# Two attention-and-feed-forward blocks on one core: the first unit of weights alone split and multiplied beside the attention, with the heads' work laid out anew

## The chip, the cores and the metric

The kernel runs on one core of a Trainium2 chip. The time is device time in microseconds, the median of several executions. The engines are named as in the profile: PE (TensorE), PEld (its weight loads), DVE (VectorE), ACT (ScalarE), POOL (GpSimd), and SP, whose queue issues the transfers.

## What is computed

Causal attention over 2 batches of 12 heads, 448 tokens and 64 channels each, then two feed-forward blocks on the 896 tokens by 768 channels that come out of it. The weights arrive as 64-bit floating point numbers. Shortened:

```
scores = scale * matmul(q, k.T);  scores = where(upper triangle, -1e9, scores)
attn = softmax(scores);  x = matmul(attn, v)            # heads side by side: 896 x 768
x = (silu(x @ w_gate) * (x @ w_val)) @ w_out            # 768 -> 1536 -> 768
h = x @ w_in;  out = maximum(h, 0)**2 @ w_out2          # 768 -> 2048 -> 768
```

## The kernel before, in words

**Weights.** The weights are cut into 68 units of 128 rows by 768 columns: g and v by turns (gate and value, 12 of each), then o, h and f. A unit is loaded as 64-bit words (`load_w`, tile wraw) by a transfer on SP, and split by `split_w` into a high part whi and a low part wlo, each a type that PE multiplies in one pass. The split has nine steps, each one instruction: step 0 the absolute value of the high words (ACT, tile wa), step 1 a clamp (DVE), 2 a shift (DVE), 3 a merge with the sign (DVE), 4 rounding to whi (ACT), 5 a mask (DVE, tile wr), 6 a scaling of the low words (DVE), 7 a subtraction (DVE), 8 the sum that gives wlo (DVE). There are two buffers of wa, one of wr, three pairs of whi and wlo.

**Three multiplications.** `mm3` multiplies one block of a unit with one block of tokens three times: high by high, high weight by low token part, low weight by high token part. Given two batches it does each of the three for both batches before it goes to the next. Tokens' parts are ahi and alo. A unit on one batch is 18 multiplications, on both 36.

**Attention.** The heads go in 12 pairs. For a pair `stage_at` transposes q and k on PE and `stage_copy` copies them on ACT; `score_mm` multiplies them on PE in two halves; `score_max` (DVE) and `score_exp` (ACT), four chunks to a head; `guard` (POOL), `recip` (DVE), `normalise` (POOL, four chunks; DVE for the first two heads); `transpose_p` (PE, in two groups), `transpose_out` (one group on ACT, one on DVE); `values` (PE), and its result goes to ahi (`channels_hi`, ACT) and alo (`channels_lo`, DVE).

**Order.** Every engine works through its instructions in the order in which they are written. In the attention that order comes from a planner: `attention_plan` lists the operations with an engine, a cost of the planner's own, what each follows and which buffers it takes, and `Plan.run` places them one by one by their start and a rank. The ranks are the head's number plus an offset from the table RANK. The constant NEARLY says how many units of weights the plan holds whole: for each the load (W), the nine steps (J), the multiplications on the first batch (G, `early_mm`, tile early) and a copy of their result to SBUF (GC, `early_out`, on ACT). Of one unit more, the load and steps 0 to 3 are in the plan.

**Behind the attention** the order is the written one. The main loop calls `gate_or_val` for g and v by turns: for the first NEARLY units on the second batch alone, since the first is there already, for all others on both batches. Before it uses a unit, `unit` sees to it by `split_to` that this one and the next are split. The steps of one unit and the first steps of the next stand by turns there:

```
elif n == NEARLY:
    split_w(n, 4)
after = start_w()
if after is not None:
    split_w(after, 0)
...
for z, y in ((5, 1), (6, 2), (7, 3), (8, 4)):
    split_w(n, z)
    if after is not None:
        split_w(after, y)
```

Between them `follow_up` puts the instructions that finish earlier units: sigmoids, products, splits of results.

Of the kernel before, what the change touches and what calls it, by code (L numbers as in the profile page):

```python
# [23 lines left out]
MASKED = -8.0e9  # L24

C = 112
NEARLY = 2


RANK = {  # L30
# [4 lines left out]
}  # L35

QUEUED = 1130
# [6 lines left out]
class Warmth:  # L44

    W, LEAST, FROM = 10240 / 3, 3060, 24000
# [19 lines left out]
class Plan:  # L66
# [9 lines left out]
    def add(self, key, engine, cost, after=(), takes=(), uses=(), rank=0, later=0, cols=0):  # L76


        later += 200 if engine == "PE" else 120
        self.ops[key] = (engine, cost, tuple(after), tuple(takes), rank, later, cols)  # L80
        for t in (*takes, *uses):
            self.users.setdefault(t, []).append(key)
# [69 lines left out]
def attention_plan(NP, NPAIR, NC, S, U, KD, rank=RANK):  # L152
# [59 lines left out]

    for n in range(NEARLY + 1):
        r = rank["J"] + n
        raw, a, b, ws = ("wraw", n), ("wa", n), ("wr", n), ("ws", n)
        add(("W", n), "SP", 2200, [("LD", n, 1)], [raw], [], rank["W"] + 2 * n, 2500)
        for z in range(9 if n < NEARLY else 4):
            engine, cost, takes, uses = (
# [4 lines left out]
            add(("J", n, z), engine, cost, [("J", n, z - 1)] if z else [("W", n)], takes, uses, r)  # L223
        if n >= NEARLY:
            continue
# [33 lines left out]
def tile_attention_moe_moe(ctx, tc, q, k, v, w_gate, w_val, w_out, w_in2, w_out2, out):  # L259
# [131 lines left out]
    def start_w():  # L391
        n = state["start"]
        if n < NU:
            load_w(n + 3)
            state["start"] += 1
            return n

    def split_to(upto):

        while state["split"] < min(upto, NU):  # L400
            n = state["split"]
            if state["start"] == n:
                for z in range(5):
                    split_w(start_w() if z == 0 else n, z)
            elif n == NEARLY:
                split_w(n, 4)
# [213 lines left out]
    def gate_or_val(kind, m, bs):  # L620
        hi, lo = unit(kind, m, 0)
        pss = {b: bank(kind) for b in bs}
        for kk in range(KD):
            c = slice(kk * 128, (kk + 1) * 128)
            mm3(pss, hi[:, c], lo[:, c], x_hi[kk], x_lo[kk], kk == 0, kk == KD - 1)
        return pss
# [42 lines left out]
    with tc.manual_schedule():  # L669
# [43 lines left out]
        for m in range(KF1):  # L713
            for kind in "gv":
                ps = gate_or_val(kind, m, [1] if n < NEARLY else [0, 1])
                if n < NEARLY:
                    ps[0] = early[n]
# [118 lines left out]
```

## Time and profile before

| | |
|---|---|
| median of 3 runs | 604.18 us (604.11 to 604.2) |
| profiled execution | 604.23 us, of which the span from the first to the last instruction is 602.1 |
| PE busy | 594.5 us, 99% of the span |
| DVE busy | 473.5 us, 79% |
| ACT busy | 284.1 us, 47% |
| POOL busy | 89.9 us, 15% |

Times in the profile count from the start of the span. The attention takes the first sixth of it: the last value product begins at 95.68 us. An instruction's duration begins when it is started and ends when its result is there, so that two neighbours on one engine can overlap; the distance from one start to the next is then what an instruction takes of its engine.

### The profile page before, as it was taken

How to read it: one execution, taken by the hardware profiler on the slowest of the kernel's cores; microseconds unless marked ns; L12 is line 12 of the kernel's file. 1: busy time of each engine (PE TensorE's matmuls, PEld its weight loads, DVE VectorE, ACT ScalarE, POOL GpSimd, SP SyncE). 2: the span in 40 equal slices, each digit the busy share in tenths (PEclk: the TensorE clock that was granted, in tenths of full speed). 3: DMA queues.
4: the chain of work that ended last, by engine and by line, in shares of the span. 5: the costliest groups of instructions: out<-in, count | busy, mean ns of one | idle time of the engine just before them, and what ended most of it. 6: DMA issues, size and time to landing. Idle time of an engine off the chain costs nothing.

```text
span 602.1 us, 8832 instructions
## 1 busy us (share of the span) xinstructions
PE 594.5 (99%) x3258; PEld 531.4 (88%) x3259; DVE 473.5 (79%) x839; ACT 284.1 (47%) x556; POOL 89.9 (15%) x154
## 2 busy tenths in 40 slices
PE   8999999999999999999999999999999999999997
PEld 5676667999999999999999999999999999999997
DVE  4878983999999999999977776888888888649741
ACT  5999983433333333333422224666666642222301
POOL 4566871211111111111000000000000000000000
PEclk9999999999999999999999999999999999999999
DMA  8795210333333333333433333333333335334202
GB/s 169 162 243 116 75 54 1 106 104 106 104 106 106 104 106 108 106 111 115 139 104 106 104 106 104 107 106 104 106 104 106 104 107 157 105 132 138 85 1 93
DMA packets 80779, 65.06 MB, mean 108 GB/s; under 512 B 34912, under 2 KB 76640, under 8 KB 80736
## 3 DMA queue, kind: packets, MB, share of 16 engines
q1 hardware_dynamic: 79808, 64.27, 36.6%
q8 instruction: 26, 0.43, 0.3%
q10 hardware_dynamic: 928, 0.23, 0.2%
q14 instruction: 17, 0.14, 0.1%
HBM read 61.73 MB, written 2.75 MB: 107 GB/s over the span
## 4 chain that ended last, share of the span: by engine, by line
PE 84%; ACT 0%; issue 0%; ACTq 0%
PE o L786 19%; PE h L616 7%; PE h L614 7%; PE h L618 7%; PE y L614 5%; PE y L618 5%; PE y L616 5%; PE g L618 5%; PE v L618 5%; PE v L614 5%; PE g L614 5%; PE v L616 5%; PE g L616 5%; PE early L614 0%; PE early L616 0%; PE early L618 0%
## 5 line engine op out<-in xcount | busy, mean ns | idle before, releaser
L374 ACT ACTIVATE whi<-wa 128x768 fp32r<-128x768 f32 x68 | 57.6, 847 | 177.3 <-DVE wa L371 134.8
L786 PE MATMUL o<-whi,b 128*128 128x384 f32 x336 | 85.6, 334 | 0.0
L362 DVE TENSOR_SCALAR wa<-wa 128x768 f32<-128x768 f32 x68 | 41.2, 606 | 46.4 <-ACT wa L359 46.4
L371 DVE SCALAR_TENSOR_TENSOR wa<-wraw,wa 128x768 uint32<-128x768 uint32 x68 | 75.6, 1112 | 0.0
L359 ACT ACTIVATE wa<-wraw 128x768 f32<-128x768 f32 x68 | 61.6, 906 | 17.8 <-DVE wlo L387 17.8
L387 DVE TENSOR_TENSOR wlo<-wa,wr 128x768 fp32r<-128x768 f32 x68 | 65.4, 961 | 0.1
L384 DVE TENSOR_TENSOR wa<-wa,whi 128x768 f32<-128x768 f32 x68 | 64.6, 951 | 0.4 <-ACT whi L374 0.4
L381 DVE SCALAR_TENSOR_TENSOR wr<-wraw,wr 128x768 f32<-128x768 uint32 x68 | 64.6, 951 | 0.1
L786 PEld LDWEIGHTS o<-whi,b 128*128 128x128 f32 x336 | 60.8, 188 | 0.0
L786 PE MATMUL o<-wlo,b 128*128 128x384 f32 x168 | 56.1, 334 | 0.0
L614 PE MATMUL h<-b,whi 128*128 128x448 f32 x192 | 55.2, 368 | 0.0
L618 PE MATMUL h<-b,wlo 128*128 128x448 f32 x192 | 55.2, 368 | 0.0
L709 POOL TENSOR_TENSOR b<-u,b 128x448 fp32r<-128x448 f32 x24 | 29.0, 1208 | 159.9 <-ACT b L708 159.9
L554 POOL TENSOR_SCALAR P<-P,st 128x448 f32<-128x448 f32 (+1 forms) x88 | 48.7, 571 | 11.6 <-DVE st L546 4.8
L536 ACT ACTIVATE P<-P,st 128x320 f32<-128x320 f32 (+2 forms) x96 | 47.7, 500 | 3.1 <-DVE st L530 1.5
L530 DVE CUSTOM_DVE_ANT_0 P<-s,mask 128x448 f32<-128x448 f32 (+2 forms) x96 | 35.2, 410 | 13.9 <-PE s L515 12.7
L614 PE MATMUL y<-b,whi 128*128 128x448 f32 x144 | 41.4, 368 | 0.0
L616 PE MATMUL y<-b,whi 128*128 128x448 f32 x144 | 41.4, 368 | 0.0
L618 PE MATMUL y<-b,wlo 128*128 128x448 f32 x144 | 41.4, 368 | 0.0
L614 PE MATMUL g<-ahi,whi 128*128 128x448 f32 x138 | 40.2, 368 | 0.0
L614 PE MATMUL v<-ahi,whi 128*128 128x448 f32 x138 | 40.2, 368 | 0.0
L618 PE MATMUL g<-ahi,wlo 128*128 128x448 f32 x138 | 40.1, 368 | 0.0
(98 smaller groups left out, 1152.4 us busy)
## 6 DMA issues: line engine op xcount, KB each, us to landing
wraw<-in_moe_w_out_dram SPq DMA_DIRECT2D x28, 768.0 KB, 4.4
wraw<-in_moe_w_in_dram SPq DMA_DIRECT2D x16, 768.0 KB, 4.6
wraw<-in_moe_w_gate_dram SPq DMA_DIRECT2D x12, 768.0 KB, 4.4
wraw<-in_moe_w_val_dram SPq DMA_DIRECT2D x12, 768.0 KB, 4.4
raw<-in_q_dram SPq DMA_DIRECT2D x24, 112.0 KB, 3.0
out_dram<-osb SPq DMA_DIRECT2D x14, 192.0 KB, 1.9
raw<-in_k_dram SPq DMA_DIRECT2D x22, 112.0 KB, 2.8
v<-in_v_dram SPq DMA_DIRECT2D x24, 96.0 KB, 2.7
```

The source lines that it names most:

```text
L359: nc.scalar.activation(out=af, in_=high.bitcast(F32), func=AF.Abs)
L371: nc.vector.scalar_tensor_tensor(out=a, in0=high, scalar=0xC0000000, in1=a, op0=ALU.bitwise_and, op1=ALU.bitwise_or)
L374: nc.scalar.activation(out=split_t[n][0], in_=af, func=AF.Copy)
L381: nc.vector.scalar_tensor_tensor(out=rf, in0=low, scalar=2.0 ** -52, in1=rf, op0=ALU.mult, op1=ALU.mult)
L384: nc.vector.tensor_tensor(out=af, in0=af, in1=split_t[n][0].bitcast(F32), op=ALU.subtract)
L387: nc.vector.tensor_tensor(out=split_t[n][1], in0=af, in1=r[0].bitcast(F32), op=ALU.add)
L536: nc.scalar.activation(out=a, in_=a, func=AF.Exp, scale=-1.0, bias=st(0), accum_out=st(1))
L554: (nc.vector if n_on_dve(h) else nc.gpsimd).tensor_scalar(out=o, in0=a, scalar1=st(2), scalar2=1.0, op0=ALU.mult, op1=ALU.mult)
L614: nc.tensor.matmul(out=pss[b][:, :S], lhsT=hi, rhs=mhi[:, halves(b)], start=first, stop=False)
L616: nc.tensor.matmul(out=pss[b][:, :S], lhsT=hi, rhs=mlo[:, halves(b)], start=False, stop=False)
L618: nc.tensor.matmul(out=pss[b][:, :S], lhsT=lo, rhs=mhi[:, halves(b)], start=False, stop=last)
L786: nc.tensor.matmul(out=pss[t][:, :N], lhsT=a[f][:, tk], rhs=w[:, c], start=f + n == 0, stop=f == KF2 - 1 and n == 2)
```

## The change

NEARLY goes from 2 to 1, and the table RANK gets other offsets. So the plan holds unit 0 whole and unit 1 up to step 3, in place of units 0 and 1 whole and unit 2 up to step 3. Unit 1's multiplications on the first batch, the copy of their result, and its steps 4 to 8, leave the plan, as do unit 2's load and steps 0 to 3. The main loop then multiplies unit 1 with both batches. Shortened to the two constants and the first line of the table:

```diff
-NEARLY = 2
+NEARLY = 1
...
-    "RA": 190.39, "AT": 2.52, "AC": -48.88, "S": -178.65, "SI": -278.69, "VJ": -5.38,
+    "RA": 348.64, "AT": 2.02, "AC": -96.22, "S": -383.35, "SI": -307.19, "VJ": -150.17,
```

In the rows below, lines of the changed kernel are lower by one. On DVE, the end of the attention and the first instructions behind it, before: COPY is the transposed probabilities' second group, alo4 and alo5 are `channels_lo` of pairs 10 and 11, wa_1213 and wr_1532 are unit 2's tiles, wa_1526 is unit 3's.

```order
L584 COPY pt_1374<-pt_1369 128x512
L371 SCALAR_TENSOR_TENSOR wa_1213<-wraw_608,wa_1213 128x768
L605 TENSOR_TENSOR alo4_87<-x_1378,ahi4_81 128x448
L584 COPY pt_1406<-pt_1400 128x512
L605 TENSOR_TENSOR alo5_88<-x_1415,ahi5_82 128x448
L377 TENSOR_SCALAR wr_1532<-wa_1213 128x768
L362 TENSOR_SCALAR wa_1526<-wa_1526 128x768
L381 SCALAR_TENSOR_TENSOR wr_1532<-wraw_608,wr_1532 128x768
L367 TENSOR_SCALAR wa_1526<-wa_1526 128x768
L704 TENSOR_TENSOR sg_1528<-early_1436,sg_1528 128x448
L384 TENSOR_TENSOR wa_1213<-wa_1213,whi_1521 128x768
L371 SCALAR_TENSOR_TENSOR wa_1526<-wraw_1498,wa_1526 128x768
```

The same place after: wa_786 and wr_1471 are unit 1's tiles, wlo_1461 its low part, wa_1469 is unit 2's.

```order
L545 RECIPROCAL st_150<-st_150 128x4
L604 TENSOR_TENSOR alo4_87<-x_1354,ahi4_81 128x448
L583 COPY pt_1358<-pt_1370 128x512
L583 COPY pt_1389<-pt_1383 128x512
L604 TENSOR_TENSOR alo5_88<-x_1398,ahi5_82 128x448
L376 TENSOR_SCALAR wr_1471<-wa_786 128x768
L361 TENSOR_SCALAR wa_1469<-wa_1469 128x768
L380 SCALAR_TENSOR_TENSOR wr_1471<-wraw_612,wr_1471 128x768
L366 TENSOR_SCALAR wa_1469<-wa_1469 128x768
L383 TENSOR_TENSOR wa_786<-wa_786,whi_1460 128x768
L370 SCALAR_TENSOR_TENSOR wa_1469<-wraw_1463,wa_1469 128x768
L386 TENSOR_TENSOR wlo_1461<-wa_786,wr_1471 128x768
```

The merge of unit 2 (L371 on wa_1213) stood among the last heads and is gone from there, and the steps that stand right behind alo5 now make unit 1's low part, with unit 2's clamp second among them.

On ACT at the same place before, from the last head's second copy on: ahi5 is `channels_hi` of pair 11, whi_1521 is unit 2's high part.

```order
L586 ACTIVATE pt_1406<-pt_1393 128x512
L600 ACTIVATE ahi5_82<-x_1415 128x448
L659 ACTIVATE early_1436<-early_1348 128x448
L659 ACTIVATE early_1453<-early_1432 128x448
L374 ACTIVATE whi_1521<-wa_1213 128x768
L359 ACTIVATE wa_1526<-wraw_1498 128x768
```

And after: whi_1460 is unit 1's high part, wa_1469 unit 2's absolute value.

```order
L585 ACTIVATE pt_1389<-pt_1376 128x512
L599 ACTIVATE ahi5_82<-x_1398 128x448
L658 ACTIVATE early_1415<-early_1335 128x448
L373 ACTIVATE whi_1460<-wa_786 128x768
L358 ACTIVATE wa_1469<-wraw_1463 128x768
L373 ACTIVATE whi_1479<-wa_1469 128x768
```

One copy of an early result is left of two, and the rounding behind it is that of unit 1.

On PE, from the last early multiplication of the first unit's first batch on, after: g_1482 is unit 0 on the second batch, v_1522 and v_1523 are unit 1 on the two batches, whi_1460 and wlo_1461 its parts.

```order
L615 MATMUL g_1482<-alo5_88,whi_795 128x448
L617 MATMUL g_1482<-ahi5_82,wlo_796 128x448
L613 MATMUL v_1522<-ahi0_77,whi_1460 128x448
L613 MATMUL v_1523<-ahi0_77,whi_1460 128x448
L615 MATMUL v_1522<-alo0_83,whi_1460 128x448
L615 MATMUL v_1523<-alo0_83,whi_1460 128x448
L617 MATMUL v_1522<-ahi0_77,wlo_1461 128x448
L617 MATMUL v_1523<-ahi0_77,wlo_1461 128x448
L613 MATMUL v_1522<-ahi1_78,whi_1460 128x448
L613 MATMUL v_1523<-ahi1_78,whi_1460 128x448
```

Before, 18 multiplications of unit 1 on the first batch (early_1432, with whi_920 and wlo_921) stood between those of unit 0 on the first batch (ahead) and on the second (g_1502, behind):

```order
L616 MATMUL early_1348<-alo5_88,whi_905 128x448
L618 MATMUL early_1348<-ahi5_82,wlo_906 128x448
L614 MATMUL early_1432<-ahi0_77,whi_920 128x448
L616 MATMUL early_1432<-alo0_83,whi_920 128x448
...
L618 MATMUL early_1432<-ahi5_82,wlo_921 128x448
L614 MATMUL g_1502<-ahi0_77,whi_905 128x448
L616 MATMUL g_1502<-alo0_83,whi_905 128x448
```

What moved is the first batch of unit 1: it stands behind g now, beside the second.

## Rows read from the trace of the kernel before

**Rows 1.** The page: busy time, granted clock in 40 slices, the chain that ended last.
```profile
PE 594.5 (99%) x3258; PEld 531.4 (88%) x3259; DVE 473.5 (79%) x839; ACT 284.1 (47%) x556; POOL 89.9 (15%) x154
...
PEclk9999999999999999999999999999999999999999
...
PE 84%; ACT 0%; issue 0%; ACTq 0%
```

**Rows 2.** Busy time by stage; behind PE, PEld, DVE, ACT, POOL: clock, DMA.
```profile
16.00:84.00 68.00, 66.40 (x545) 47.59 (x544) 56.25 (x214) 64.99 (x210) 45.64 (x96) 1.00 0.57 141
...
98.00:112.00 14.00, 14.00 (x70) 12.72 (x69) 7.76 (x12) 6.89 (x10) 0.00 (x0) 1.00 0.18 56
```

**Rows 3.** Waits of ACT from 12 to 90 us: total, times, longest.
```profile
ACT pt L586 <- PE pt L571: 1.1, 3, 0.5
...
ACT P L536 <- DVE st L530: 0.2, 1, 0.2
```

**Rows 4.** Timeline of ACT at 77 us: start, duration, instruction.
```profile
77.19 0.89 ACT L359 ACTIVATE wa<-wraw 128x768 f32<-128x768 f32 x1
78.04 0.67 ACT L536 ACTIVATE P<-P,st 128x448 f32<-128x448 f32 x1
```

**Rows 5.** Timeline of ACT: the last exponential's sum.
```profile
89.23 0.19 ACT L536 ACTIVATION_READ_ACCUMULATOR P<-P,st 128x1 f32 x1
```

**Rows 6.** Timeline of POOL, the last three heads.
```profile
84.48 1.83 POOL L554 TENSOR_SCALAR P<-P,st 128x448 f32<-128x448 f32 x4 [0.38 <-DVE st L530]
...
87.34 2.86 POOL L554 TENSOR_SCALAR P<-P,st 128x448 f32<-128x448 f32 x4 [0.49 <-DVE st L546]
90.29 0.22 POOL L541 TENSOR_SCALAR st<-st 128x4 f32<-128x4 f32 x1
90.89 2.68 POOL L554 TENSOR_SCALAR P<-P,st 128x448 f32<-128x448 f32 x4 [0.38 <-PE pt L571]
```

**Rows 7.** Timeline of DVE beside POOL's last group.
```profile
91.82 1.17 DVE L371 SCALAR_TENSOR_TENSOR wa<-wraw,wa 128x768 uint32<-128x768 uint32 x1
```

**Rows 8.** Timeline of PE: last transposes, first and 25th multiplication behind the values.
```profile
93.33 0.44 PE L564 MATMUL pt<-ident,P 128*128 128x128 f32 x2 [0.28 <-POOL P L554]
...
97.56 0.47 PE L614 MATMUL early<-ahi,whi 128*128 128x448 f32 x1
...
102.62 0.37 PE L614 MATMUL g<-ahi,whi 128*128 128x448 f32 x1
```

**Rows 9.** Timeline of ACT behind the attention.
```profile
99.10 0.55 ACT L659 ACTIVATE early<-early 128x448 f32<-128x448 f32 x1 [0.87 <-PE early L618]
102.82 0.55 ACT L659 ACTIVATE early<-early 128x448 f32<-128x448 f32 x1 [3.17 <-PE early L618]
103.26 0.84 ACT L374 ACTIVATE whi<-wa 128x768 fp32r<-128x768 f32 x1
103.99 0.90 ACT L359 ACTIVATE wa<-wraw 128x768 f32<-128x768 f32 x1
```

**Rows 10.** Timeline of DVE behind the attention.
```profile
104.92 0.56 DVE L362 TENSOR_SCALAR wa<-wa 128x768 f32<-128x768 f32 x1 [5.57 <-ACT wa L359]
105.40 0.95 DVE L381 SCALAR_TENSOR_TENSOR wr<-wraw,wr 128x768 f32<-128x768 uint32 x1
106.27 0.55 DVE L367 TENSOR_SCALAR wa<-wa 128x768 uint32<-128x768 uint32 x1
106.81 0.62 DVE L704 TENSOR_TENSOR sg<-early,sg 128x448 f32<-128x448 f32 x1
107.35 0.95 DVE L384 TENSOR_TENSOR wa<-wa,whi 128x768 f32<-128x768 f32 x1
108.22 0.95 DVE L371 SCALAR_TENSOR_TENSOR wa<-wraw,wa 128x768 uint32<-128x768 uint32 x1
109.09 0.62 DVE L704 TENSOR_TENSOR sg<-g,sg 128x448 f32<-128x448 f32 x1
109.63 0.95 DVE L387 TENSOR_TENSOR wlo<-wa,wr 128x768 fp32r<-128x768 f32 x1
```

5 rows, old and new, of the table RANK are left out of this document.

## The prediction

> **What bounds the kernel now.** I read the page first. TensorE (PE) is busy for 594.5 of 602.1 us, and the chain that ended last is PE nearly throughout, with the three-fold multiplications of the feed-forward part on top [rows 1]. Busy PE rows overlap, so I then read the busy time by stage [rows 2]. From 98 us on PE has no gap at all: the multiplications follow one another every 0.21 us (24 of them between 97.56 and 102.62 [rows 8]). Their number is the same before and after, so behind the attention a microsecond on the path can come only from a new wait. In the attention it is different. From 16 to 84 us ScalarE (ACT) is busy for 64.99 of 68 us and PE for 66.40, VectorE (DVE) for 56.25 [rows 2]. ACT waits for others only 2.6 us in all between 12 and 90 us (five rows of waits, of which the first and the last are shown) [rows 3]. So two engines share the pace of the attention, and ACT is the one that loses work.
>
> **What the change takes out.** Before, units 0 and 1 were split wholly during the attention, and unit 2 up to step 3. After it is unit 0 wholly and unit 1 up to step 3. Nine instructions leave: on ACT one absolute value (step 0) and one rounding (step 4), on DVE steps 5 to 8 of one unit and 1 to 3 of another. On ACT, measured from one start to the next, the absolute value takes 78.04 - 77.19 = 0.85 us [rows 4] and the rounding 103.99 - 103.26 = 0.73 us [rows 9], 1.58 together. On DVE it is 0.56 + 0.95 + 0.55 + 0.95 + 0.95 + 0.95 us [rows 10] and one mask like the 0.55 one, some 5.5 us. The 18 multiplications of unit 1 on the first batch are not removed: they stood behind the last value product, where PE was never idle, and now stand in the same stage with the second batch's. They cost and save nothing. The first early copy on ACT stays; the second goes from a place where ACT was idle.
>
> **Steady part.** ACT's 1.58 us come off the path if PE can follow. PE's work per pair of heads is unchanged, so the lower bound of the gain is 0: PE at 98% busy follows no faster. The upper one is 1.58 plus all of ACT's 2.6 us of waits, 4.2. I take 1.6, because ACT's share and its few waits are the nearest rows: the removed time goes, the waits stay. The new order of heads has no row that prices it, and stands inside these bounds.
>
> **Drain.** The last exponential's sum was read at 89.23 + 0.19 = 89.42 [rows 5], but GpSimd (POOL) took up the last head only at 90.29, 0.87 us later, since its four normalisations of head 22 lasted from 87.34 to 90.20. They took 2.86 us, those of head 23 2.68, those of head 21 only 1.83 [rows 6]. Behind the long ones steps of the split ran on DVE, such as the 1.17 us step at 91.82 [rows 7]; in the changed order no step of the split stands between head 20's maxima and the end of the attention. At 1.83, head 22's would end at 89.17, before 89.42: of the 0.87 I count 0.8 as gained. Head 23's gain another 2.68 - 1.83 = 0.85. The bounds are 0 and 1.65. The last transposes, which began at 93.33 [rows 8], would then be ready at 91.7; PE has pair 10's values and half a transpose to put in front of them, so I take 1.4.
>
> **The new wait.** Everything is counted from the start of the multiplications behind the last value product, 97.56 before [rows 8]. PE then has 6 of unit 0's first batch and 18 of its second, as many as the 24 from 97.56 to 102.62: 5.06 us. Unit 1 begins there with four that need only its high part, 4 x 0.21 = 0.83, and at 5.89 us wants the low part. That is made in this order: ACT copies the early result (99.10, so 1.54), then rounds unit 1, then takes the absolute value of unit 2. Only then can DVE go on, since the second row in its queue, the clamp of unit 2, waits for that value, and all of unit 1's remaining steps stand behind it. From the copy to the clamp it took 104.92 - 102.82 = 2.10 us before [rows 9, 10], so the clamp starts at 3.64. Then come clamp 0.48, scale 0.87, shift 0.54, subtraction 0.87, merge 0.87 and the last sum 0.95 (starts to starts, without the two products between them, the last by its length) [rows 10]: 4.58, together 8.22 us. PE stands still for 8.22 - 5.89 = 2.3 us; a tenth either way on each of the nine steps makes it 1.4 to 3.2. The same chain was harmless before, because unit 1's two batches covered it: the low part of unit 2 was there at 109.63 + 0.95 = 110.58. The next unit after the change has the stall itself as cover, and I see no second wait. Unit 2's load moves on SP behind the last loads of the heads, but its wraw buffer is the third of three and free, and the values of pair 6, for which the last of those loads waits, lie five pairs ahead of the end. What is queued behind the clamp on DVE is only the split; behind the waiting multiplication, all of PE.
>
> **Sum.** 1.6 + 1.4 - 2.3 = 0.7 us less. The profiled execution took 604.23 us (602.1 span and 2.1 around it; the median of the runs is 604.18), which gives **603.5 us**. What a measurement of this kernel can tell from no change is about 0.2%, 1.2 us, so this is no change.
>
> **The rivals.** First, the new order also removes ACT's waits: 4.2 + 1.4 - 2.3 = 3.3 us less, 600.9. For it speaks that 5.5 us leave DVE, and with them the delays of maxima that ACT waits for; against it that PE has to find over 4 us where its own busy time leaves 1.6 of 68.
> Second, and on the other side, PE alone sets the pace and the attention ends when it did: then the 2.3 us of the wait stand alone, 606.5. It decides as soon as the attention ends less than 1.1 us earlier. PE's 98% speaks for it, the 0.87 us that POOL was late against it.
> Third, the granted clock. It is at the full 2.4 GHz in every slice and stage here [rows 1, 2], but in none of them does PE stand still for as much as 2.3 us. If it falls to its lower level, 1.2 GHz, what is worked at that level takes twice as long. No row has it, so I bound the stretch by the wait: with 2.3 us spent at the lower level 1.2 us are lost, with 2.3 us of full-speed work done at it 2.3, which gives 604.7 to 605.8.
> The Trainium skill has this as a rule in "TensorE: Matmul & The Clock Gate", section "Why this matters for your kernels": gaps of an idle PE between bursts of multiplications are to be avoided, as the clock is then throttled to half. It speaks against the change; no stretch of this trace shows it.
> Fourth, the change brings no wait, because unit 1's low part comes in time after all: 3.0 us less, 601.2. The order of DVE's queue speaks against it.
>
> **How the numbers follow.** Forecast 0.42, waits also gone 0.20, attention no shorter 0.15, clock 0.18, no wait 0.05. Faster by over 0.2%: the first and the fourth rival and a little of the forecast's own spread, 0.28 in all. Slower: the second, and half of the third, 0.24. Within: 0.48. The forecast's own range is 602.3 (drain 1.65, wait 1.4) to 604.6 (drain 1.2, wait 3.2). The range over the cases goes from 601.2 to 606.0 and leaves out part of the first rival and most of the second, about 2 in 10.
>
> **What would show it.** In the changed profile: the first wait of PE on wlo of unit 1, some 5.9 us behind the last value product, of 2 to 2.6 us; the value product itself ending about 3 us earlier than 97.6; POOL's last two groups of normalisations at 1.8 to 2.1 us; ACT at 95% or more from 16 to 80 us; the granted clock 1.00 behind the wait. Wrong would be: no shorter attention (the steady term), or a wait that is missing or twice as long (DVE slowed, or the weights of unit 2 loaded late, since their load is now queued on SP behind the last heads' loads), or a second wait at unit 2.

## The result

The changed kernel took 596.72 us (median of 6 runs, 596.21 to 602.22), the kernel before on the same chip 604.14: a ratio of 0.989, 95% interval 0.9856 to 0.9926. The forecast was 603.5 with a range from 601.2, so the time lies below it. A second series of 12 runs of the same kernel (below) had its median at 602.21. The runs of the two series fall into groups, 596 to 597 and 602 to 604.6, with one run at 600.72 between them, and most of what follows is about what separates them.

The profiled execution of the changed kernel belongs to the upper group: 602.22 us, span 600.2. The page's busy times and clock, which answer to [rows 1]:

```profile
PE 592.2 (99%) x3256; PEld 530.5 (88%) x3257; DVE 474.2 (79%) x839; ACT 283.0 (47%) x555; POOL 85.8 (14%) x154
...
PEclk9999999999999999999999999999999999999999
```

The same two stretches as [rows 2]:

```profile
16.00:84.00 68.00, 67.49 (x568) 49.63 (x567) 57.17 (x227) 65.53 (x218) 45.53 (x101) 1.00 0.53 130
...
98.00:112.00 14.00, 11.85 (x58) 10.45 (x57) 13.15 (x20) 6.30 (x8) 0.00 (x0) 1.00 0.37 117
```

In the attention PE and ACT are both fuller than before. PE started 568 instructions in these 68 us, where it had started 545, so the 98% at which it was busy before were not its limit. Behind it PE has lost 2.15 us of 14, where it had none idle. The timelines show where each term went. First ACT, which answers to [rows 5, 9]: the last exponential's sum, the early copy, the rounding of unit 1 and the absolute value of unit 2.

```profile
86.15 0.19 ACT L535 ACTIVATION_READ_ACCUMULATOR P<-P,st 128x1 f32 x1
...
94.78 0.55 ACT L658 ACTIVATE early<-early 128x448 f32<-128x448 f32 x1 [0.87 <-PE early L617]
95.22 0.84 ACT L373 ACTIVATE whi<-wa 128x768 fp32r<-128x768 f32 x1
95.95 0.90 ACT L358 ACTIVATE wa<-wraw 128x768 f32<-128x768 f32 x1
```

POOL's last groups of normalisations, as [rows 6]:

```profile
84.16 1.84 POOL L553 TENSOR_SCALAR P<-P,st 128x448 f32<-128x448 f32 x4 [0.38 <-PE pt L573]
86.43 0.22 POOL L540 TENSOR_SCALAR st<-st 128x4 f32<-128x4 f32 x1 [0.43 <-ACT P L535]
87.03 1.84 POOL L553 TENSOR_SCALAR P<-P,st 128x448 f32<-128x448 f32 x4 [0.38 <-DVE st L545]
```

DVE from the clamp of unit 2 to the last sum of unit 1, as [rows 10]:

```profile
96.88 0.56 DVE L361 TENSOR_SCALAR wa<-wa 128x768 f32<-128x768 f32 x1 [1.85 <-ACT wa L358]
...
100.43 0.95 DVE L386 TENSOR_TENSOR wlo<-wa,wr 128x768 fp32r<-128x768 f32 x1
```

And PE, as [rows 8]: the last value products, the first multiplication behind them, and the one that waits.

```profile
91.36 1.95 PE L592 MATMUL x<-pt,v 128*64 128x448 f32 x16
93.24 0.47 PE L613 MATMUL early<-ahi,whi 128*128 128x448 f32 x1
...
98.71 0.57 PE L615 MATMUL v<-alo,whi 128*128 128x448 f32 x2
101.44 0.68 PE L617 MATMUL v<-ahi,wlo 128*128 128x448 f32 x2 [2.15 <-DVE wlo L386]
```

The last exponential ends at 86.34, before at 89.42: 3.08 us earlier. From there to the first multiplication behind the values it takes 6.90 us (8.14 before): 1.24 less. Then comes the wait, 2.15 us. The sum, 3.08 + 1.24 - 2.15 = 2.2, agrees with what this execution gained on that of before, 604.23 - 602.22 = 2.0. So the steps of the prediction account for the upper group, at 602.2. They do not account for the other 5.5 us, down to 596.7.

### The profile page after: what moved, and what is told of

It reads as the page before. It is cut to its first block, busy times and chain, and to the rows that moved or that the text cites. A ratio compares the mean times of both kernels' runs of the same rounds, so it can differ in the third digit from the quotient of the medians.

```text
span 600.2 us, 8841 instructions
## 1 busy us (share of the span) xinstructions
PE 592.2 (99%) x3256; PEld 530.5 (88%) x3257; DVE 474.2 (79%) x839; ACT 283.0 (47%) x555; POOL 85.8 (14%) x154
## 4 chain that ended last, share of the span: by engine, by line
PE 95%; DVE 2%; POOL 1%; DMA 1%; issue 0%; ACT 0%; SPq 0%; ACTq 0%; POOLq 0%
PE o L785 19%; PE h L615 7%; PE h L617 7%; PE h L613 7%; PE v L617 5%; PE y L615 5%; PE y L613 5%; PE y L617 5%; PE v L613 5%; PE v L615 5%; PE g L613 5%; PE g L617 5%; PE g L615 5%; PE s L514 4%; PE x L592 3%; PE pt L570 2%
## 5 line engine op out<-in xcount | busy, mean ns | idle before, releaser
L535 ACT ACTIVATE P<-P,st 128x448 f32<-128x448 f32 (+2 forms) x96 | 47.7, 503 | 3.3 <-DVE st L529 1.9
L553 POOL TENSOR_SCALAR P<-P,st 128x448 f32<-128x448 f32 (+1 forms) x88 | 44.2, 522 | 10.2 <-DVE st L545 5.3
L617 PE MATMUL v<-ahi,wlo 128*128 128x448 f32 x144 | 41.4, 369 | 2.2 <-DVE wlo L386 2.2
L615 PE MATMUL v<-alo,whi 128*128 128x448 f32 x144 | 41.4, 368 | 0.0
```

Of the source, the lines that this page charges most:

```text
L535: nc.scalar.activation(out=a, in_=a, func=AF.Exp, scale=-1.0, bias=st(0), accum_out=st(1))
L553: (nc.vector if n_on_dve(h) else nc.gpsimd).tensor_scalar(out=o, in0=a, scalar1=st(2), scalar2=1.0, op0=ALU.mult, op1=ALU.mult)
L615: nc.tensor.matmul(out=pss[b][:, :S], lhsT=hi, rhs=mlo[:, halves(b)], start=False, stop=False)
L617: nc.tensor.matmul(out=pss[b][:, :S], lhsT=lo, rhs=mhi[:, halves(b)], start=False, stop=last)
```

## The experiments

### Which of the two times is the changed kernel's?

The same kernel once more, without an edit, for a profile of the other group.

> The changed kernel once more, unedited, because its profiled execution (602.22 us) and five unprofiled ones (596.2 to 596.9) differ by some 5.6 us. Theory A: the slow one is a rare execution that loses 5.6 us at one place, so a second profile shows about 596.5 us, with the last value product some 5 us earlier than 93.2 us or with no wait of PE at unit 1. Theory B: the time lost is spread over the feed-forward part, so that a second profile at 596.5 us has the same attention and the same wait of 2.2 us, and multiplications that follow one another 1% faster than every 0.207 us. Theory C: profiling itself costs it in this program, and the second profile is at 602 too, while the timed runs are at 596.5.

Measured: median 602.21 (596.59 to 604.55, 12 runs), ratio 0.994, 0.991 to 0.9979. Five runs at 596.6 to 597.0, one at 600.72 (the profiled one), six at 603.7 to 604.6. The profiled one has the wait again, with 2.15 us at 101.36, so what separates it from the first profiled one (602.22) is not the wait. The execution at 600.72 shows both kinds of progress, in the busy time of two stretches of 40 us in which PE does nothing but the same multiplications of 448 columns:

```profile
110.00:150.00 40.00, 40.00 (x199) 37.07 (x198) 36.25 (x50) 14.51 (x22) 7.83 (x6) 1.00 0.33 102
200.00:240.00 40.00, 40.00 (x196) 36.32 (x195) 36.23 (x50) 14.90 (x23) 7.02 (x6) 1.00 0.35 115
```

PE is busy for all 40 us in both, at the full clock, with 199 multiplications in the first and 196 in the second. Counted from start to start, one takes 202.7 ns or 206.7 ns. An example for each, first the profiled changed kernel, whose first and last row in a stretch of 20 us are 97 multiplications apart: (219.75 - 199.70) / 97 = 206.7 ns.

```profile
199.70 0.37 PE L617 MATMUL g<-ahi,wlo 128*128 128x448 f32 x1
...
219.75 0.57 PE L613 MATMUL v<-ahi,whi 128*128 128x448 f32 x2
```

And the kernel of the next experiment, 99 multiplications apart: (219.71 - 199.64) / 99 = 202.7 ns.

```profile
199.64 0.36 PE L618 MATMUL g<-ahi,wlo 128*128 128x448 f32 x1
...
219.71 0.57 PE L616 MATMUL g<-alo,whi 128*128 128x448 f32 x2
```

I call these the long and the quick pace. From 101.95, where PE goes on behind the wait, to 480.15, where the stage with 384 columns begins (173.3 ns in every profile), there are some 1830 multiplications: 1830 x 4.0 ns = 7.3 us between the paces. The profile of before and the first one of after have the long pace throughout. In the one above the quick pace begins behind the wait at 101 us, breaks off at 167, where a weight load has waited 0.19 us for DVE, is back from 181 on, and ends for good at 197, where one has waited 0.22 us. Some 400 multiplications at the quick pace, 4.0 ns less each, are 1.6 us, and this execution is 1.5 us faster than the first. So theory B holds in kind: the time lies in the row of multiplications. Theory C does not hold, since a profiled execution at 596.97 follows below.

### The units and the order apart

The kernel before with `NEARLY = 1` and its old table RANK:

```diff
-NEARLY = 2
+NEARLY = 1
```

> The kernel before with NEARLY = 1 and its own table of ranks: one part of the change alone. By my forecast's terms (ACT loses 1.6 us, POOL is freed at the end for 1.4, PE waits 2.3) some 603.5 us; if the gain of the change lies in the new order of the heads, about 604 to 606, with PE waiting 2 to 2.5 us for wlo of unit 1; if it lies in the work taken out of the attention, 600 or less.

Measured: 602.27 (597.74 to 605.16, 12 runs), ratio 0.9957, 0.9932 to 0.9982. Six runs at 602.2 to 602.9, two at 605.2, four at 597.7 to 597.9. The first multiplication behind the values is at 94.76, 2.8 us earlier than before, and the wait is 2.23 us. The profiled run (597.94) has the quick pace from 94.76 on, ahead of the wait. Behind the wait the granted clock falls. Busy time and, behind POOL, clock by stretches of 2 us:

```profile
100.00:102.00 2.00, 0.70 (x4) 0.31 (x2) 2.00 (x4) 0.00 (x0) 0.00 (x0) 1.00 0.38 104
102.00:104.00 2.00, 1.07 (x5) 1.01 (x6) 1.58 (x4) 1.92 (x3) 0.00 (x0) 0.97 0.82 289
104.00:106.00 2.00, 2.00 (x7) 1.80 (x6) 2.00 (x4) 1.99 (x3) 0.00 (x0) 0.50 0.00 0
106.00:108.00 2.00, 2.00 (x8) 1.80 (x8) 2.00 (x3) 0.15 (x1) 0.00 (x0) 0.68 0.72 201
108.00:110.00 2.00, 2.00 (x11) 1.85 (x11) 1.97 (x4) 1.30 (x2) 0.00 (x0) 1.00 0.55 197
```

0.50 is the lower level, 1.2 GHz, and a pair of multiplications that takes 0.57 us elsewhere takes 0.95 us there (104.57 on PE). From start to start one takes 373 ns there against 202.7 ns, 1.8 times as long. That is the third rival: it comes in some executions and not in others. In the upper group of the changed kernel the runs with a mean clock of 0.996 or 0.997 take 603.7 to 604.6 and the one at 1.0 takes 602.2: 1.5 to 2.4 us. In the lower group of the first series the same difference is only 0.4 to 0.7 us (596.7 to 596.9 against two runs at 596.2); why it is less there, no profile shows.

Now the new table alone, with `NEARLY = 2`.

> The kernel before with NEARLY = 2 and the new table of ranks: the other part alone. No wait of PE on wlo is expected, since unit 1 is split in the attention. If the gain lies in the new order, the last value product starts near 91 to 93 us and the time is 598 to 600; if it lies in the work taken out, it is 604 or more.

Measured: 604.39 (597.52 to 605.03, 11 runs), ratio 0.9995, 0.9975 to 1.0015: no change. Yet the last exponential is read at 85.54, earlier than in the whole change. The gain is lost on POOL, where the last two groups of normalisations are long although ACT is done:

```profile
85.69 2.77 POOL L553 TENSOR_SCALAR P<-P,st 128x448 f32<-128x448 f32 x4 [0.38 <-PE pt L570]
88.55 0.22 POOL L540 TENSOR_SCALAR st<-st 128x4 f32<-128x4 f32 x1
89.15 2.64 POOL L553 TENSOR_SCALAR P<-P,st 128x448 f32<-128x448 f32 x4 [0.38 <-PE pt L570]
```

On DVE, steps of the split stand beside them (a last sum at 85.45, a shift at 86.29, a merge at 90.65). PE waits 2.2 us for POOL at the attention's end, the clock is at 0.88 from 84 to 98 us, and the last values begin at 96.40, later than before. Part of the loss is the clock's: eight of the eleven runs, the profiled one among them, have a mean clock of 0.996 or 0.997 and take 603.8 to 605.0; the three at 0.999 or 1.0 take 597.5, 602.5 and 603.0. So the new order brings the exponentials forward, and in the profiled run nothing of that reaches PE's last values without the removed steps.

To test that DVE's work is what lengthens POOL's, the changed kernel with four sums of two inputs on DVE beside the last group (the sums are used nowhere):

```diff
+            if key == ("R", NH - 1):
+                junk = early_p.tile([128, S], F32, tag="junk", name="junk")
+                for _ in range(4):
+                    nc.vector.tensor_tensor(out=junk, in0=mask, in1=mask, op=ALU.add)
```

> The changed kernel with four sums of two SBUF tiles (128x448, into a tile that nobody reads) on DVE, behind the last reciprocal, where DVE is idle for 2.4 us. If DVE's two-input steps are what stretched POOL's normalisations before (2.86 and 2.68 against 1.84 us), the last head's normalisations take 2.6 to 2.9 us, PE waits for POOL ahead of the last transposes, and the last values start 0.7 to 1.0 us later than 91.3. If POOL was late for another reason, they stay at 1.84 and the values at 91.3.

Measured: 596.97 (profiled), 601.21, 600.71, 601.25, ratio 0.9931, 0.9909 to 0.9953. On POOL the last group took 3.14 us in place of 1.84, beside the sums on DVE (86.61 to 89.82):

```profile
86.86 3.14 POOL L553 TENSOR_SCALAR P<-P,st 128x448 f32<-128x448 f32 x4 [0.38 <-DVE st L545]
```

The last values began at 91.75, only 0.39 us later than in the changed kernel and less than the 0.7 to 1.0 expected: PE waited for POOL for only 0.34 us there. That DVE's instructions lengthen POOL's is shown by this; that it costs PE as much as POOL is not. The Trainium skill says the same in "SBUF — State Buffer", section "Who interferes with whom": a DVE instruction with two inputs in SBUF contends with a GpSimd instruction that reads there. The trace agrees, with 1.84 against 3.14 us.

### The wait

First the wait taken away: the last five steps of unit 1 in one piece, with no step of unit 2 between them.

```diff
             elif n == NEARLY:
-                split_w(n, 4)
+                for z in range(4, 9):
+                    split_w(n, z)
+                state["split"] += 1
+                continue
```

> The changed kernel, with unit 1's steps 4 to 8 written in one piece ahead of unit 2's first steps, so that no step of unit 1 stands behind the clamp that waits for ACT. The low part should be there about 4.4 us behind the last value product, ahead of the 5.9 at which PE wants it: no wait there and 2.2 us less than the changed kernel. If the wait is not what costs the time (it is given back later by another, at unit 2), the same time as the changed kernel.

Measured: 600.44 (599.83 to 601.21, 5 runs), ratio 0.9942, 0.993 to 0.9953. The wait at unit 1 is gone and unit 2 comes too late instead, by a third as much:

```profile
107.36 0.67 PE L620 MATMUL g<-ahi,wlo 128*128 128x448 f32 x2 [0.80 <-DVE wlo L386]
```

Behind that wait the quick pace holds to 196 us, but PE catches up with DVE: once in every pair of units, six times and 14.78 us apart, a weight load waits 0.29 to 0.31 us for wlo. Behind the sixth, at 196.06, the long pace returns.

Second, the steps put where DVE has nothing to do, ahead of the last value product's result:

```diff
+            if key == ("XH", NP - 1):
+                split_w(1, 4)
+            if key == ("XL", NP - 1):
+                for z in range(5, 9):
+                    split_w(1, z)
+                state["split"] += 1
             work[key[0]](*key[1:])
```

> The changed kernel with unit 1's steps 4 to 8 written ahead of the last pair's ahi and alo, where ACT and DVE are idle for 2.9 us: unit 1's low part is then there before PE needs it, and unit 2 keeps its interleaved order. No wait of PE on wlo at unit 1 or 2, and no fall of the clock: 600.0 us where the multiplications keep the slower pace throughout, less where they take the faster one, 592.6 at the least. If the wait only moves on to unit 2, 601 to 602.

Measured: 599.66 (599.53 to 600.1, 5 runs), ratio 0.9927, 0.9914 to 0.9939. No wait of PE from 80 us to the end, a mean clock of 0.999, the long pace throughout. So at the long pace the wait is worth 602.2 - 599.7 = 2.5 us. None of these five runs was at 596, where over half of those with the wait are.

Third, a wait in the kernel before, far from the change: the last sum of unit 22 four times over.

```diff
-            nc.vector.tensor_tensor(
-                out=split_t[n][1], in0=af, in1=r[0].bitcast(F32), op=ALU.add)
+            for _ in range(4 if n == 22 else 1):
+                nc.vector.tensor_tensor(
+                    out=split_t[n][1], in0=af, in1=r[0].bitcast(F32), op=ALU.add)
```

> The kernel before, in which unit 22's last sum (step 8) is written four times instead of once, with the same result: one wait of PE of about 1.1 us at 260 us, in a kernel that has none behind the attention and that shows one pace there (0.2067 us a multiplication). Theory W: a wait draws the pace of the multiplications anew, 0.2067 or 0.2027. Then the executions split: some near 605.0 (the wait alone), some near 600.6 (1080 multiplications of 448 columns are left, at 4 ns each). Rival L: the faster pace comes with NEARLY = 1 (its layout, its order of units). Then all executions are at 605.0, none below 604.

Measured: 604.26 (601.62 to 607.02, 12 runs), ratio 1.0002, 0.9979 to 1.0026, in two groups, five runs at 601.6 to 602.0 and five at 605.5 to 606.1; the other two, 603.01 and 607.02, have a fallen clock (0.997). The groups are 4 us apart, as 1080 multiplications at the two paces would be. In the order of their list the twelve runs go from one group to the other every time, with 603.01 counted to the lower group and 607.02 to the upper one, so what chooses is hardly chance alone. The kernel before does not show such groups: of the 75 runs of it beside these experiments 72 lie between 603.2 and 604.7, the other three at 598.8, 598.9 and 601.9. In the profiled run (603.01) PE waits 2.43 us at 261.20, where 1.1 was expected. From 216 us to the wait it has the long pace, behind it the quick one. But the quick pace was there before, too, from the attention's end at 98 us to 169 and from 184 to 214, with four waits of a weight load for DVE of 0.20 to 0.30 us on the way and one of 0.30 us at the end of either stretch. Two rows 54 multiplications apart, (123.88 - 112.94) / 54 = 202.6 ns, and a stretch behind the wait:

```profile
112.94 0.57 PE L619 MATMUL g<-ahi,wlo 128*128 128x448 f32 x2
...
123.88 0.56 PE L619 MATMUL v<-ahi,wlo 128*128 128x448 f32 x2
...
300.00:340.00 40.00, 40.00 (x200) 37.06 (x199) 31.00 (x44) 13.12 (x18) 0.00 (x0) 1.00 0.36 118
```

So a wait can be where PE passes from the long pace to the quick one, and the quick one can also begin where the attention ends, without any wait of PE behind the attention.

### The pace without a wait

The kernel before with one multiplication of 64 columns ahead of gate unit 11. Its result is overwritten by the next one.

```diff
         pss = {b: bank(kind) for b in bs}
+        if (kind, m) == ("g", 11):
+            nc.tensor.matmul(
+                out=pss[0][:, :64], lhsT=hi[:, :128], rhs=x_hi[0][:, :64], start=True, stop=True)
```

> The kernel before with one more multiplication of 64 columns ahead of unit 22, whose result the next one overwrites: PE's stream is shifted by some 0.05 us without any wait. If any irregularity draws the pace anew, the executions split into 604 and 600; if it takes a wait for another engine, all stay at 604.

Measured: 600.02 (599.79 to 600.3, 5 runs), ratio 0.9931, 0.9919 to 0.9943. One instruction more makes the kernel before 4.1 us faster, in every run, without any wait. PE around it:

```profile
258.06 0.57 PE L616 MATMUL v<-alo,whi 128*128 128x448 f32 x2
258.48 0.57 PE L618 MATMUL v<-ahi,wlo 128*128 128x448 f32 x2
258.89 0.19 PE L624 MATMUL g<-ahi,whi 128*128 128x64 f32 x1
258.92 0.64 PE L614 MATMUL g<-ahi,whi 128*128 128x448 f32 x2
259.39 0.57 PE L616 MATMUL g<-alo,whi 128*128 128x448 f32 x2
259.80 0.57 PE L618 MATMUL g<-ahi,wlo 128*128 128x448 f32 x2
```

The pace is 206.7 ns up to there and 202.7 ns from there to 478 us, where the stage with 384 columns begins. Some 1070 multiplications x 4.0 ns = 4.3 us, which is about the gain.

As a control, the same with 448 columns, as wide as its neighbours (`:448` for `:64`).

> The kernel before with one multiplication more ahead of gate unit 11, as in the run with 64 columns (600.0), but with 448 columns like its neighbours. If any instruction more turns the pace, 600.2. If it takes one that is out of step with the others, a 448-column one leaves the row as it was: 604.4.

Measured: 603.32 (597.9 to 604.52, 12 runs), ratio 0.999, 0.9965 to 1.0015: no change, and the long pace on both sides in the profile. Two runs of 12 were at 597.9 and 598.8. So an extra instruction by itself does not turn the pace at this place, and the short one does. That it does so by being out of step with the row is a guess: two widths were tried, the wide one at one place.

The same instruction in the kernel without the wait, ahead of gate unit 5 (`("g", 5)`), at 165 us:

> The changed kernel with steps 4 to 8 of unit 1 in the gap before the last value product (599.7 us, no wait, 206.7 ns from one multiplication to the next throughout), and one multiplication of 64 columns more ahead of gate unit 5, at about 165 us, whose result the next one overwrites. If one such instruction turns the pace for good, as it did in the kernel before at gate unit 11 (604.2 to 600.0), some 1520 multiplications up to 480 us take 4.0 ns less each: 6.1 us, 593.6. If it does so only at that place or in that kernel, 599.7. Threat: at the quick pace PE does a pair of units in 14.59 us and DVE splits one in 14.77, so that 1.3 us of lead last just about seven pairs; if PE meets DVE it waits 0.1 to 0.2 us a pair, and the pace may change back: then 594 to 597.

Measured: 594.12 (593.68 to 598.14, 6 runs), ratio 0.9875, 0.9837 to 0.9912. Four runs are at 593.7 to 594.1. The two at 598 are not explained. Ahead of gate unit 1, at 105.6 us:

> The same with the one multiplication ahead of gate unit 1, at 105.6 us. The pace alone would give 599.7 less 1810 multiplications x 4.0 ns = 7.2: 592.5. DVE's lead there is 0.9 us, which lasts five pairs at 0.18 us each, to about 178 us; from there PE waits on wlo, 0.18 us a pair for the six pairs that are left (593.6 if the pace stays), or the first such wait changes the pace back to 206.7 ns, and 598 to 599 remains.

Measured: 598.27 (594.21 to 598.59, 6 runs), ratio 0.99, 0.9865 to 0.9934. The profiled run shows the threat that was named: PE catches up with DVE. The weight loads that wait for it, two of six:

```profile
179.79 0.30 PEld L617 LDWEIGHTS g<-ahi,wlo 128*128 128x128 f32 x2 [0.20 <-DVE wlo L386]
194.56 0.30 PEld L617 LDWEIGHTS g<-ahi,wlo 128*128 128x128 f32 x2 [0.29 <-DVE wlo L386]
```

They are 14.77 us apart, as are the others up to 254: a pair of units then takes what DVE takes for it. Between the waits the pace stays the quick one; behind the last, at 253.69, it is the long one, and from 268 on the quick one again. The four runs at 598.1 to 598.6 lie where the expectation put a pace that goes back at the first such wait; none of them was profiled. And with a second one of 64 columns ahead of gate unit 9, beside that ahead of gate unit 5:

> The first of these with a second such multiplication of 64 columns ahead of gate unit 9, at about 223 us. If an irregularity turns the pace over, whichever it was, the quick pace lasts from 165 to 223 us only, 1.1 us less than 599.7: 598.5. If the quick pace is where the row settles, the second changes nothing: 593.6, as with one.

Measured: 593.85 (593.76 to 593.95, 6 runs), ratio 0.9847, 0.9822 to 0.9872. The second does not turn the quick pace back: the row stayed in it each time. This is the fastest version, 1.5% below the kernel before and the same in all six runs.

### Does the pace explain the two groups, and what chooses it?

The changed kernel, its wait included, with the 64 columns ahead of gate unit 11:

> The changed kernel, its wait included, with one multiplication of 64 columns more ahead of gate unit 11, at about 259 us. If the pace of the multiplications is what separates its executions of 602 to 604.5 us from those of 596 to 597, the slow ones all turn quick there and lose some 1070 x 4.0 ns = 4.3 us, as the kernel before did: 597.9 and 599.8 (clock fallen), the quick ones stay at 596 to 597, and none is above 600.5. If something else separates them, executions of 602 to 604.5 us remain.

Measured: 596.49, 596.55, 596.62 and 599.49, 599.68, 599.84, ratio 0.9905, 0.9886 to 0.9925. As expected, nothing is above 600.5: the upper group with a fallen clock, 603.7 to 604.6 before, has come down by over 4 us. The profiled execution, 596.49, is a kind of its own. Its clock is at 1.00, and it has the quick pace from the wait to 167 us, where a weight load waits 0.19 us, then the long one, and the quick one again from the inserted multiplication on; without that it would be like the one at 600.72.

The lower group is seen in the run with sums on DVE, profiled at 596.97. Its PE has the instructions of the changed kernel, a wait of 2.23 us and a fallen clock behind it, and from there to the stage with 384 columns the quick pace throughout:

```profile
200.00:240.00 40.00, 40.00 (x199) 37.08 (x198) 36.26 (x49) 14.51 (x22) 7.02 (x6) 1.00 0.35 109
300.00:340.00 40.00, 40.00 (x199) 37.08 (x198) 32.27 (x46) 13.00 (x18) 0.00 (x0) 1.00 0.37 118
```

And where the clock has fallen, the two groups of the second series, 596.6 to 597.0 and 603.7 to 604.6, are some 7.3 us apart, as much as 1830 multiplications at the two paces. The pace is what separates the two.

The changed kernel with the 64 columns ahead of the wait, at 98.4 us:

> The changed kernel with the multiplication of 64 columns ahead of unit 1 (value unit 0), at 98.3 us and so ahead of the 2.15 us wait. It makes the pace quick before the wait. If the pace is fixed ahead of the wait and passes through it unchanged, all executions take 596 to 597. If the wait draws it anew, there are two groups as without the multiplication: 596 to 597, and 602 to 604.5.

Measured: 596.19, 596.28, 596.55, 597.55, 600.52, 600.73 and 603.92, ratio 0.9912, 0.988 to 0.9944. One run is as long as the upper group and three lie between, so the short multiplication at this place does not fix the pace of the whole row. Whether it made the pace quick ahead of the wait can't be read: only four multiplications stand between. In the profiled run (596.55) the quick pace holds from the wait to the end of the row, and the clock falls behind the wait:

```profile
101.53 1.00 PE L617 MATMUL v<-ahi,wlo 128*128 128x448 f32 x2 [2.07 <-DVE wlo L386]
```

It fell behind a wait of 2.07 us here and stayed at 1.00 behind 2.15 us in three profiles, so the length of the wait does not decide it by itself. In the profile of the second experiment and in that of the run with sums on DVE the quick pace was there before the wait, so the wait is not its only origin.

## Why the prediction was wrong

**Steady part: right in kind, too small.** Forecast 1.6 us, measured 3.08 (bounds 0 to 4.2). With the old table the units alone end the last exponential at 87.67, 1.75 us earlier than before, close to the 1.6; the new order adds 1.3. That is the term which the prediction put at nothing: "The new order of heads has no row that prices it". ACT's busy time up to its last exponential, before and after:

```profile
0.00:89.42 89.42, 86.02 (x670) 60.74 (x671) 68.65 (x275) 80.20 (x254) 57.19 (x124) 1.00 0.58 138
...
0.00:86.34 86.34, 83.88 (x671) 60.34 (x673) 66.25 (x270) 77.76 (x252) 54.71 (x125) 1.00 0.57 134
```

It fell by 2.4 us, from 80.20 to 77.76, and by as much with the units alone (77.79); the rest of the time, in which ACT is idle, is 9.2 us before, 9.9 with the units alone and 8.6 after. So the removed work gave 2.4, more than the 1.6 of the two instructions, and the order decides whether ACT gains or loses idle time beside it; why the busy time fell by 0.9 more than the 1.6 stays open. The first rival did not come true: ACT waits 2.5 us from 12 us to the end of its exponentials, where it had waited 2.6. The premise of the second, that PE at 98% can follow no faster, did not hold.

**Drain: right.** 1.24 us measured against 1.4. POOL's last groups went from 2.86 and 2.68 to 1.84 us, as the prediction had them. The run with sums added on DVE shows the mechanism, the run with the new order alone shows that without the removed steps the gain is lost there.

**New wait: right.** 2.15 us forecast as 2.3, from 6.05 us behind the last value product (forecast 5.9), on wlo of unit 1, in one place only.

**Clock: a rival that came true in part.** The prediction priced a fall behind the wait at 1.2 to 2.3 us; it was found at 0.50 behind a wait of 2.23 us, and in the upper group the runs that have it take 1.5 to 2.4 us longer. The prediction's "twice as long" was measured as 1.8 times. The rule that the prediction named from the Trainium skill ("TensorE: Matmul & The Clock Gate", section "Why this matters for your kernels") is borne out by that fall; but behind 2.15 us in the changed kernel's first profile the clock stays at 1.00, so for a gap of this size the trace agrees in some executions only.

**The step that failed** is in the first part: "the multiplications follow one another every 0.21 us", their number is the same, "so behind the attention a microsecond on the path can come only from a new wait". The 0.21 us were 206.7 ns, and not a constant. The same instructions, all operands there, the clock at 1.00, also run at 202.7 ns, and in two profiles (600.72 and 596.49) PE passes from the long pace to the quick one at the change's own wait. In the kernel before nothing disturbs the row from 98 to 480 us, and it keeps the long pace in nearly every run. No rival had it, and a PE that is busy in every slice hid it.

So of the 7.4 us between the medians of the first series, 1.9 (604.1 to 602.2) follow from the steps of the prediction, and 5.5 are what the quick pace leaves in the five other runs. At 7.3 us between the paces that is an estimate: none of the five was profiled, and part of the 7.3 goes to the fallen clock, which three of them have, or to waits of weight loads for DVE. That the second series has its median at 602.21, inside the forecast's range, is no merit of the prediction: it stands between two groups. Of all 18 runs of the changed kernel 10 ended below 597. Without its wait and at the long pace, which the times of all five runs fit, the change is worth 4.5 (599.7).

## What to carry to other kernels

Where one engine sets the end with a long row of equal instructions, divide the time between two far starts by their count, in several stretches and in every profile: a 2% difference in pace is invisible in busy shares and is worth more here than every wait. When a kernel's runs fall in two groups, take a profile of each group before explaining the median, and try to hold the pace equal (here by one short instruction) before comparing two versions. Here a wait of 2 us cost its length, in some executions 1.5 to 2.4 us of clock as well, and in some the row behind it ran at another pace.

## What the runs showed of the hardware that was not expected

- The row of weight loads and 448-column multiplications has two steady paces at the full clock, 206.7 and 202.7 ns; with 384 columns only 173.3 ns was seen, in every kernel.
- One multiplication of 64 columns turned the long pace into the quick one (5 of 5 runs before gate unit 11), a second one left it, one of 448 columns left the long one in 10 of 12 runs. Waits of a weight load for DVE of 0.2 to 0.3 us ended the quick pace or left it: at 0.19 and 0.22 us it ended (second series), at 0.29 to 0.31 us it stayed five times and ended at the sixth (the run with steps 4 to 8 in one piece).
- The granted clock fell to 0.50 behind waits of PE of 2.07, 2.23 and 2.43 us and stayed at 1.00 behind 2.15 us in three other profiles.
- Why PE has two paces, and what chooses between them behind a wait or at the attention's end, stays open: no view here shows it.
- Four normalisations on POOL took 1.84 us at 84.16 in the changed kernel, where DVE only copied out of PSUM and formed alo, and 2.64 to 3.14 us beside steps of the split or sums of two SBUF tiles.
